# Backward recurrence of a memory transformer: the gradient of O regrouped from SBUF to SBUF, the memory rows' dP in one product, V's part moved to its own block

## The chip, the cores and the metric

One core of a Trainium2 chip. The time is the device time of one execution in microseconds; the time before is the median of three runs.

## The reference, cut to what matters

The kernel returns the output of a block and its gradients with respect to the input, the initial memory, four attention weights and the MLP's weights and biases. The attention part is recurrent: 2048 rows are cut into 64 segments of 32, and each is preceded by 8 memory rows that the segment before has produced.

```python
for s in range(n_seg):                                   # 64
    h = concat([mem, xs[s]], axis=1)                     # 8 + 32 rows of 512
    q, k, v = (einsum('btd,dhe->bhte', h, W) for W in (Wq, Wk, Wv))   # 32 heads of 128
    p = softmax(where(mask, q @ k.T * scale, -1e9))
    o = einsum('bhte,hed->btd', p @ v, Wo)
    mem, out = o[:, :8], o[:, 8:]                        # mem goes into segment s + 1
y = x + out + mlp(layernorm(x))
# returned: y and the gradients by x, mem0, Wq, Wk, Wv, Wo, w1, b1, w2, b2 for a given grad_out
```

The mask lets the 8 memory rows see all 40 rows, and lets row t of the segment see the memory rows and the rows up to its own. In the backward pass the gradient of `mem` goes from segment s to segment s - 1, so the segments run from 63 down to 0, one after another.

## The kernel before

There are four stages: the MLP with its gradients and the layer norm; a first recurrence (forward), up to about 1190 us; a second recurrence (the backward pass of attention), from there to about 2250 us; and the weight gradients with the gradient through the layer norm to the end. The change lies in the second.

**Layout.** A tile has 128 partitions. A "natural" tile (`gN`, `qN`, `kN`, `xs`) has 1024 columns of bf16 and holds four groups of 8 heads: partitions 32j to 32j + 31 are 32 rows (of one segment, or the memory rows of a whole block) for the heads 4i + j, and the columns are 8 heads of 128. Four segments make a block (`SPB` = 4, `TC` = 16 blocks). `s` is a segment, `b = s // 4` its block, `v = s % 4` its place; within a block v runs 3, 2, 1, 0.

**On the chain.** `chain(s)` takes a segment: the gradient of O by the heads, `gN` (projection with Wo, "gO"), its transpose, dP = gO times V (line L1930; V's transpose with the memory's columns is tile `VT`), the softmax's backward pass on VectorE, and three products (`part_bd` 2, 1, 0 for the gradients of V, K and Q), each written to DRAM (`S_GN`) and multiplied by Wv, Wk, Wq into one sum (`dh_part`, L1770). The sum is evicted (`R_A`), and a small matmul (L1985) puts its first 8 rows into the next segment's input `gT`.

**Off the chain.** The queries of the memory rows are handled for the 32 memory rows of a block at once. `l_pre(b)` loads the block's tiles and makes their gradient of O (`gLN`), their dP (L1805, against the memory rows' own keys, tile `VTL`, and the segment's first rows, `VTM`), their softmax gradient (`dSL`, `dSTLL`), and the gradient of Q, which goes to DRAM (`S_GNL[0]`). It is issued when the block before it is at v = 2. `l_post(b)`, issued one block later, reads dQ back, makes the gradients of K (part 1) and V (part 2) and their sum with the weights. For these two it needs rows of all four segments of the block regrouped so that 128 partitions are 4 segments x 32 rows of one head group. That regrouping goes over DRAM: `chain` stores `gN` to `S_GON` (256 KB a segment), and `l_post` loads it back by `quad_rows`, head group by head group, into the four tiles `xs`; it does the same with `S_Q`, and with the padded probabilities `S_PL` and `S_DSL` (64 KB each) into `ys`. Line L1857 multiplies the memory rows' own part, L1870 the regrouped rows.

**Order.** A planner (`_Beat`) writes out the order of all instructions of the recurrence from a table of due times, `_BWD`: one table for the middle blocks, one for the first and one for the last. The numbers decide in which order the operations stand in each engine's queue, and for evictions and copies which engine takes them; nothing waits for a due time itself. Nearly all DMAs of this stage are issued on SP's queue, in the order of the table: an issue that waits holds up those behind it. Many tiles live in parts of larger ones, so the trace shows `XK`, `XN`, `XA`, `XH` for several of the names here (`gN` is in `XA`; the tiles `xs` are in `XN`; `LT0`, `LT1`, the odd `kLN` and `VTL` are in `XK`).

Of the kernel before, what the change touches and what calls it, by code (L numbers as in the profile page):

```python
# [17 lines left out]
P = 128  # L18
# [180 lines left out]
        11817202, 10472800, 15851602, -17692400, -106800, -10764000, 216000, -12492400, 3623200, 6284000, -528797,  # L199
        -546000, -2857200, -480000, -481200, 8879250, 1958400, 3563600, 3428400, 3358800, 10119849, 10143660,  # L200
        10143673, 10758308, 10758321, 6099600, 4994800, 2060400, 541200, 4580802, 7385202, 7385602, 8326802, 8824402,
        9103200, 9060400, 12611600, 12610400, 13626861, 13626873, -4334000, -3086798, -8438400, -12837600, -319597,
        -13471197, -16186000, 938000, 14389648, 14697884, 15015510, 15015520, 15015546, 15015568, 14915540, 14915552,
        14915565, 15155304, 15155317, 16495172, 12582691, 12582703, 14416771, 12582715, 12178775, 12178787, 12178799,
        13008887, 15015532, 15015557, 15015580, 15015593, 15246942, 16495186, 15246952, 15246964, 17158024, 17158036,
        15015664, 15015606, 16401514, 16401526, 16401538, 16401550, 16401562, 16401622, 16495198, 16495210, 17240374,
        17240386, 18255066, 17240398, 18255078, 15015619, 15015631, 15015643, 15015655, 16401575, 16401585, 16401597,
        16401611, 16944336, 16944349, 17240410, 17240423, 17240433, 17240446, 17240456, 17240517, 18235906, 18286922,
        18235916, 18235928, 18286932, 18286944, 23428480, 16401635, 16401645, 16401657, 16401671, 16401681, 16401693,
        16401707, 16401717, 17232288, 17783157, 17240469, 17240481, 17240493, 17240507, 18255090, 18255102, 18255114,  # L210
        18255127, 18255136, 18977533, 18569534, 18977546, 18569544, 18569556, 18977568, 18977580, 18977556, 19690537,
        19782597, 19690548, 19690562, 19782608, 19782622, 24547084, 17535616, 28380764, 13327536, 14420532, 24402643,
        24402655, 22194524, 19977928, -2821228, 7899676, 7373828, 3613352, -4696608, 8571312, 11740568, -69781,
        1558124, 4805860, 6352296, 7315404, 7733381, 10119800, 10119812, 10119824, 10119836, 2902029, 11447020,
        11447032, 11447044, 11447056, 11447070, 11447082, 12669054, 12669066, 13626802, 13626812, 13626824, 13626836,
        13626848, 13626884, 20930640, 20930652, 20930665, 23601096, 23601110, 24402664, 21843516, 21843528, 21843541,
        25147548, 25147561, 26802176, 18255151, 18255163, 23864939, 18255175, 20385003, 19204219, 17240531, 19148035,
        23864948, 23864961, 24748972, 24748985, 24715950, 26802190, 26947188, 27003728, 27104816, 27104828, 24749044,
        24402678, 25646686, 25646698, 25646710, 25646722, 25646734, 25646794, 26802202, 26802214, 26802226, 26802238,
        26802250, 26985338, 26802310, 24748999, 24749011, 24749023, 24749035, 25646747, 25646757, 25646769, 25646783,  # L220
        28361976, 28361989, 26802263, 26802275, 26802285, 26802297, 28614648, 28614661, 28362002, 28614710, 29609052,
        29609064, 29609076, 29609088, 30713416, 25646807, 25646817, 25646829, 25646843, 25646853, 25646865, 25646877,
        25646889, 27878264, 28843061, 27878278, 27878291, 27878301, 27878314, 26802321, 27541630, 26802335, 27083430,
        29000060, 29000073, 28843074, 29000146, 29609100, 29609112, 29609124, 29609136, 29000156, 29609149, 29609161,
        29609172, 29609210, 29609184, 29609222, 29609196, 25929872, 28805088, 21959012, 27793388, 30828719, 30828731,
        28733856, 29000084, 29609232, 29609244, 29609257, 31001308, 32005190, 32005200, 30458968, 31138912, 31138925,
        32272300, 32272313, 33163544, 29000099, 29000111, 29000123, 29000135, 28614675, 28614687, 28614699, 32237603,
        32237612, 32237637, 32237624, 32237649, 33139906, 33315202, 33982864, 33982876, 34779744, 34779756, 32237708,
        32281674, 32281686, 32281698, 32281710, 32281722, 32281734, 32281794, 33163558, 33163570, 33163582, 33163594,
        33810362, 33757294, 33810374, 32237663, 32237675, 32237687, 32237699, 32281747, 32281757, 32281769, 32281783,  # L230
        34296780, 34296793, 33163607, 33163619, 33163631, 33163641, 34923492, 34923505, 34296806, 34923566, 35592576,
        35621428, 35621440, 35621452, 35407824, 32281805, 32281817, 32281831, 32281843, 32359965, 32281853, 32281865,
# [1985 lines left out]
```

## Time and profile before

| | |
|---|---|
| time, median of three runs | 2805.26 us (2798.69 to 2806.51) |
| the profiled execution, its own time | 2806.96 us |
| its span | 2805.2 us |
| TensorE (PE) busy | 2700.5 us, 96% of the span |
| VectorE / ScalarE / GpSimd busy | 1458.3 / 1320.2 / 943.1 us |
| DMA bytes, mean rate | 606.27 MB, 216 GB/s |
| share of SP's hardware queue (q1) | 72.4% of 16 engines' span |

The page's second part cuts the span in 40 slices of 70 us; slices 18 to 32 are the second recurrence. "PEld" is TensorE's weight load, which overlaps the matmuls. A row of a wait reads: who waited, on which line, for whom, then the total in us, how often, and the longest. A row of the timeline reads: start, length, engine, line, operation, tiles written and read, count, and in brackets the idle time before it and what ended it.

### The profile page before, as it was taken

Reading aid. Unit: us, or ns where it says so; the run is one execution under the profiler, and the core shown is the slowest. Engines: PE = TensorE matmul, PEld = TensorE weight load, DVE = VectorE, ACT = ScalarE, POOL = GpSimd, SP = SyncE. Lnnn points to the kernel's source line nnn. Section 1 sums busy time; section 2 is a strip of 40 time slices with the busy share of each in tenths; the row PEclk is TensorE's granted clock in tenths of the full one; section 3 lists DMA queues with packets and bytes.
Section 4 is the critical chain, followed back from the end, with each engine's and each line's share of the span. In section 5 each row is a group of like instructions: output and inputs, shape, how many; then the busy total and the mean of one; then the engine's idle time right before and its main releaser. Section 6 shows DMA issues by size and latency. Waiting matters only on the chain.

```text
span 2805.2 us, 114167 instructions
## 1 busy us (share of the span) xinstructions
PE 2700.5 (96%) x47681; PEld 1554.6 (55%) x47681; DVE 1458.3 (52%) x4384; ACT 1320.2 (47%) x3149; POOL 943.1 (34%) x2638
## 2 busy tenths in 40 slices
PE   8999999999999999899999999999999899999999
PEld 6665555665566665665555555555555444444444
DVE  5555655555565655665656555555655402232322
ACT  4333565556565565556666666666666400000000
POOL 1102233333333333344544445454544301112211
PEclk9999999999999999999999999999999999999999
DMA  7657677877787774468999999999999898788861
GB/s 214 208 167 220 194 202 205 212 208 205 198 216 210 199 204 158 137 167 218 234 232 241 236 235 232 238 232 234 228 238 222 243 342 278 232 254 270 257 185 40
DMA packets 556392, 606.27 MB, mean 216 GB/s; under 512 B 228145, under 2 KB 357442, under 8 KB 553826
## 3 DMA queue, kind: packets, MB, share of 16 engines
q1 hardware_dynamic: 540706, 544.88, 72.4%
q0 software_dynamic: 15168, 54.08, 6.1%
q8 instruction: 374, 6.13, 1.0%
q14 instruction: 144, 1.18, 0.2%
HBM read 290.14 MB, written 272.12 MB: 200 GB/s over the span
## 4 chain that ended last, share of the span: by engine, by line
PE 48%; DMA 5%; issue 2%; DVE 2%; ACT 2%; SPq 0%; POOL 0%; POOLq 0%; DVEq 0%; ACTq 0%
PE ps L2155 14%; PE ps L1770 13%; PE ps L976 6%; PE ps L866 6%; PE ps L2158 4%; PE ps L752 3%; DMA S_GN<-XK 2%; DMA S_GON<-XA 1%; PE ps L1985 1%; PE ps L1870 1%; DMA WA<-S_GN 1%; PE ps L1930 1%; PE ps L932 1%; ACT XN L758 1%; PE ps L1857 0%
## 5 line engine op out<-in xcount | busy, mean ns | idle before, releaser
L866 PE MATMUL ps<-WA,PA 128*32 128x512 bf16 x6144 | 366.1, 379 | 4.7 <-DVE PA L1596 2.7
L2155 PE MATMUL ps<-WA,WB 128*128 128x512 bf16 x1536 | 332.3, 379 | 0.6 <-DVE gwo L756 0.6
L1770 PE MATMUL ps<-WA,XK 128*32 128x512 bf16 x5120 | 307.9, 382 | 6.5 <-DVE XK L849 6.3
L2155 PEld LDWEIGHTS <-WB 128*128 128x128 bf16 x1896 | 185.5, 98 | 224.8 <-issue 1.3
L866 PEld LDWEIGHTS <-PA 128*32 128x32 bf16 x8192 | 200.1, 96 | 194.2 <-DVE PA L1596 14.4
L992 POOL COPY BDA<-PB 32x128 bf16<-32x128 bf16 x600 | 172.8, 288 | 370.2 <-DVE PB L1566 268.4
L758 ACT CAST gwo<-ps 128x512 bf16<-128x512 f32 x64 | 33.2, 599 | 517.7 <-PE ps L2155 357.9
L758 ACT CAST XK<-ps 128x512 bf16<-128x512 f32 x379 | 211.0, 588 | 85.5 <-PE ps L976 65.2
L756 DVE CAST gwo<-ps 128x512 bf16<-128x512 f32 x64 | 40.0, 684 | 402.6 <-PE ps L2155 268.4
L1770 PEld LDWEIGHTS <-XK 128*32 128x32 bf16 x5120 | 123.1, 97 | 142.4 <-DVE XK L849 26.7
L1770 PE MATMUL ps<-WA,XN 128*32 128x512 bf16 x2560 | 173.4, 380 | 2.7 <-DVE XN L849 2.2
L2166 POOL DMA_DIRECT2D out_dram<-gwo x96 | 71.4, 751 | 296.6 <-ACT gwo L758 265.0
L758 ACT COPY XN<-ps 128x256 f32<-128x256 f32 (+2 forms) x227 | 100.8, 473 | 130.1 <-PE ps L1770 122.8
L758 ACT CAST XA<-ps 128x512 bf16<-128x512 f32 x143 | 83.4, 589 | 156.0 <-PE ps L866 131.9
L866 PE MATMUL ps<-WB,PA 128*32 128x512 bf16 x2048 | 132.5, 381 | 7.5 <-DVE PA L1988 4.3
L1648 PE MATMUL ps<-XA 128*128 128x512 bf16 x448 | 131.3, 381 | 3.3 <-DMA XA<-S_GT 2.2
L849 DVE STREAM_TRANSPOSE XK<-XK 128x256 f32<-128x256 f32 x256 | 112.0, 442 | 42.8 <-ACT XK L758 37.2
L1435 PE MATMUL ps<-WB,OT 128*32 128x256 bf16 x4096 | 132.5, 276 | 1.8 <-DVE OT L849 1.3
L998 POOL COPY BDA<-XA 32x256 bf16<-32x256 bf16 x256 | 104.5, 408 | 54.4 <-ACT BDA L992 17.7
L976 PEld LDWEIGHTS <-XK 128*128 128x128 bf16 x1536 | 94.0, 98 | 48.0 <-issue 18.0
L1435 PEld LDWEIGHTS <-OT 128*32 128x32 bf16 x4096 | 101.2, 97 | 32.6 <-DVE OT L849 19.3
L992 POOL COPY BDB<-PB 32x128 bf16<-32x128 bf16 x228 | 65.7, 288 | 157.8 <-DVE PB L1567 149.1
(310 smaller groups left out, 5467.2 us busy)
## 6 DMA issues: line engine op xcount, KB each, us to landing
S_GN<-XK SPq DMA_DIRECT2D x192, 256.0 KB
WA<-S_GN SPq DMA_DIRECT2D x160, 256.0 KB
S_Q<-qN SPq DMA_DIRECT2D x64, 256.0 KB
S_K<-kN SPq DMA_DIRECT2D x64, 256.0 KB
S_V<-vN SPq DMA_DIRECT2D x64, 256.0 KB
S_ON<-oN SPq DMA_DIRECT2D x64, 256.0 KB
XA<-S_K SPq DMA_DIRECT2D x64, 256.0 KB
XA<-S_Q SPq DMA_DIRECT2D x64, 256.0 KB
```

The source lines that it names most:

```text
L752: nc.tensor.transpose(ps_ap, in_ap, ident[base:base + k, base:base + k])
L758: nc.scalar.copy(out, in_)
L849: self.plan.add({"DVE": 0.36}, lambda e, x=x: nc.vector.transpose(dst[:, x, :, :].rearrange("p i c r -> p (i c r)").bitcast(F32).rearrange ...
L866: nc.tensor.matmul(bk()[32 * j:32 * (j + 1), :], lhsT=win(dc), rhs=Wt(dc, c0), start=(dc == 0), stop=(dc == DC - 1), tile_position=(0, 32 ...
L976: nc.tensor.matmul(bv()[:, n * P:(n + 1) * P], lhsT=B_[:, i, :, :].rearrange("p j k -> p (j k)"), rhs=X[:, i, :], start=(y == 0 and n == 0 ...
L992: self.plan.add({"ACT": 0.31, "DVE": 0.2, "POOL": 0.31}, lambda e, j=j: {"ACT": nc.scalar.copy, "DVE": nc.vector.tensor_copy, "POOL": nc.g ...
L998: self.plan.add(cost or {"ACT": 0.4, "DVE": 0.27, "POOL": 0.42}, lambda e, j=j: {"ACT": nc.scalar.copy, "DVE": nc.vector.tensor_copy, "POO ...
L1435: nc.tensor.matmul(bk()[32 * t:32 * (t + 1), :], lhsT=tq(OTt, i, j), rhs=Wo[:, JQ * i + j, h * HB:(h + 1) * HB], start=(i == 0 and j < 2), ...
L1648: A(pe(0.217, "f", 0.11), lambda e, c=c, z=z, x=x: nc.tensor.matmul(bks[x]()[:], lhsT=anT[x][:, c, :], rhs=sx[z][:], start=(c == 0), stop= ...
L1770: nc.tensor.matmul(bk()[32 * j:32 * (j + 1), :], lhsT=tq(XT, i, j), rhs=wtf(t, i, j), start=(first and i == 0), stop=(last and i == NI - 1 ...
L2155: nc.tensor.matmul(bks[n]()[:], lhsT=HNc[:, rc, dc * P:(dc + 1) * P], rhs=half_of(gns[y], hf), start=(y == 0), stop=(y == NRC - 1))
L2158: nc.tensor.matmul(bks[n]()[:], lhsT=gns[y][:, k * P:(k + 1) * P], rhs=GOc[:, rc, :], start=(y == 0), stop=(y == NRC - 1))
```

## The change

1. **The gradient of O, regrouped from SBUF to SBUF.** The DRAM tensor `S_GON` is gone. At the end of each segment four DMAs copy the four head groups of `gN` (32 partitions, 64 KB each) straight into partitions 32v to 32v + 31 of four tiles `xg`. `l_post`'s part 2 reads these. `xg` takes two of the tiles that were `xs` and two new ones, so `xs` has two tiles instead of four, used twice each for part 1. The rows of `S_PL` are loaded in the matching order (segment, row).
2. **dP of the memory rows in one product.** `VTL` and `VTM` lie beside each other and are read as one operand `VLM`; 32 matmuls with 64 columns take the place of 64 with 32.
3. **Where the parts stand.** `l_pre` is cut in pieces. `l_soft` (loads of `VTL` and `VTM`, dP, softmax gradient) is issued ahead of the last segment of the block before; `l_keys` (load of `kLN`) behind that segment; `l_query` (load of `KM`, dQ) behind the block's own first segment, and dQ's transpose is taken from the tile, not read back from DRAM. `VTL` and `kLN` have one buffer each instead of two. V's part, `l_post(b, 2)`, is issued at the end of its own block, K's part with the sum one block later, as before.
4. **A new table** `_BWD` of due times for all three kinds of block; the constant `_BWD_BEAT` is the same.

```diff
-    S_GON = dt_([TC, P, SPB, HW], BF16, "S_GON")
...
-        VTL, kLN = [tr4(XK[0], 2 * HW), tl("VTL", TR)[:]], [nat(XK[0], 4 * HW), tl("bkLN", NAT)[:]]
+        VTL, kLN = tr4(XK[0], 2 * HW), nat(XK[0], 4 * HW)
         LT0, LT1, LT2 = tr4(XK[1]), tr4(XK[0], 3 * HW), tr4(XN[3])
         VTM = LT1
+        VLM = XK[0][:, 2 * HW:4 * HW].rearrange("p (c i j r) -> p i j c r", c=2, i=NI, j=JQ)
...
-        xs = [XN[x] for x in (1, 4, 5, 7)]
-        btL = xs[3][:].bitcast(F32).rearrange("p (i k) -> p i k", i=NI)
+        xs = [XN[x] for x in (1, 4)]
+        xg = [XN[5], XN[7], tl("xg2", [P, HW]), tl("xg3", [P, HW])]
+        btL = xs[1][:].bitcast(F32).rearrange("p (i k) -> p i k", i=NI)
...
         def l_pre(b):
-            dmaT(lambda: trv(VTL[p]), lambda: S_VL[b], [], [("VTL", p)])
-            dmaT(lambda: trv(VTM), lambda: S_VM[b], [], both("LT1"))
-            sg.dma(lambda: flat(kLN[p]), lambda: S_KL[b], [], [K("kLN")], lat=3.0)
-            sg.dma(lambda: flat(KM), lambda: S_KM[b], [], both("dLN"), lat=3.0)
...
-            sg.to_T_plain("f", "gLT", gLN[p], K("gLN"), LT0, "LT0", 1)
...
-                    for c, VX in enumerate((VTL[p], VTM)):
-                        for j in range(JQ):
-                            nc.tensor.matmul(q_(bk(), j)[:, i, 32 * c:32 * c + 32], lhsT=LT0[:, i, j, :],
-                                             rhs=VX[:, i, j, :], start=(i == 0 and c == 0), stop=True,
-                                             tile_position=(0, 32 * j), skip_group_check=True)
...
+            sg.to_T_plain("f", "gLT", gLN[p], K("gLN"), LT2, "LT2", 1)
+
+        def l_soft(b):
...
+            dmaT(lambda: trv(VTL), lambda: S_VL[b], [], ["VTL"])
+            dmaT(lambda: trv(VTM), lambda: S_VM[b], [], both("LT1"))
...
+                    for j in range(JQ):
+                        nc.tensor.matmul(q_(bk(), j)[:, i, :].rearrange("p (c k) -> p c k", c=2), lhsT=LT2[:, i, j, :],
+                                         rhs=VLM[:, i, j], start=(i == 0), stop=True,
+                                         tile_position=(0, 32 * j), skip_group_check=True)
...
+            smax_bwd("L", bk, 2 * RL, PLL[p], K("PLL"), dSL[p], K("dSL"), 1, 0.71)
...
+        def l_keys(b):
+            sg.dma(lambda: flat(kLN), lambda: S_KL[b], [], ["kLN"], 0, lat=3.0)
+
+        def l_query(b):
+            sg.dma(lambda: flat(KM), lambda: S_KM[b], [], both("dLN"), lat=3.0)
+            sg.diag_own("f", [
+                (lambda r, i: q_(dSTLL, r)[:, i, 0, :], lambda r, i: q_(kLN, r)[:, i, :]),
+                (lambda r, i: q_(dSTLL, r)[:, i, 1, :], lambda r, i: q_(KM, r)[:, i, :]),
+            ], ["dSTLL", "kLN"] + both("dLN"), ("dLN", dLN), 1, True)
+            sg.dma(lambda: part_of(S_GNL[0], b, BPC), lambda: flat(dLN), both("dLN"), [])
             sg.sq_T(dLN, "dLN", LT0, "LT0", 1)
...
+                if t == 2:
+                    xx, xk = [x[:] for x in xg], [[("xg", j, v) for v in range(SPB)] for j in range(JQ)]
+                else:
+                    xx, xk = [xs[j % 2][:] for j in range(JQ)], [[("xs", 0)], ["btL"]] * 2
...
-                    sg.dma(lambda: xx[r], lambda: quad_rows(big, b, r),
-                           [(bn, s) for s in range(b * SPB, b * SPB + SPB)], xk[r], lat=3.2)
-                    sg.dma(lambda: yy[r], lambda: quad_rows(pad, b, r),
+                    if t == 1:
+                        sg.dma(lambda: xx[r], lambda: quad_rows(big, b, r), [], xk[r], lat=3.2)
+                    sg.dma(lambda: yy[r], lambda: quad_rows(pad, b, r) if t == 1 else pad[b, 32 * r:32 * (r + 1)].rearrange("r v f -> v r f"),
...
         def chain(s):
-            sg.dma(lambda: part_of(S_GON, s, SPB), lambda: flat(gN), both("gN"), [("S_GON", s)])
+            for r in range(JQ):
+                sg.dma(lambda r=r: xg[r][RA * v:RA * (v + 1), :], lambda r=r: flat(gN)[RA * r:RA * (r + 1), :], both("gN"), [("xg", r, v)], lat=3.0)
...
                 if v == SPB - 2 and b > 0:
                     l_pre(b - 1)
+                if v == 0 and b > 0:
+                    l_soft(b - 1)
                 chain(s)
                 sg.rings = {}
+                if v == 0 and b > 0:
+                    l_keys(b - 1)
                 if s > 0:
                     load(s - 1)
-                if v == SPB - 1 and b + 1 < TC:
-                    l_post(b + 1)
+                if v == SPB - 1:
+                    if b + 1 < TC:
+                        l_post(b + 1, 1)
+                    l_query(b)
+            l_post(b, 2)
             blk_out(b)
-        l_post(0)
+        l_post(0, 1)
```

More of the change, by code (lines that the diff above doesn't have):

```diff
@@ new lines, in l_soft @@
+            for y in range(4):
+                A(pe(0.11, "w"), lambda e, y=y: dp(e, y), both("LT2") + both("LT1") + ["VTL"], [bk.key])
+            smax_bwd("L", bk, 2 * RL, PLL[p], K("PLL"), dSL[p], K("dSL"), 1, 0.71)
+            A({"DVE": 0.72}, lambda e: V.transpose(dSTLL[:].rearrange("p i c k -> p (i c k)"), flat(dSL[p])),
+              [K("dSL")], ["dSTLL"])
+        def l_keys(b):
+            plan.at = (TC - 1 - b, 0)
+            sg.dma(lambda: flat(kLN), lambda: S_KL[b], [], ["kLN"], 0, lat=3.0)
@@ L2020 @@
         l_pre(TC - 1)
+        l_soft(TC - 1)
+        l_keys(TC - 1)
         pl = TC % 2
```

51 lines of the change are left out of this document (21 added, 30 removed), and 339 rows, old and new, of the table _BWD.

## The prediction

> **What bounds the kernel now.** I read the page first, then busy time by windows cut at the block borders of the second recurrence, then waits, DMA, and the timeline around the edited steps.
>
> ```profile
> span 2805.2 us, 114167 instructions
> PE 2700.5 (96%) x47681; PEld 1554.6 (55%) x47681; DVE 1458.3 (52%) x4384; ACT 1320.2 (47%) x3149; POOL 943.1 (34%) x2638
> DMA  7657677877787774468999999999999898788861
> ```
>
> TensorE is busy 96% of the span, and the DMA row stands at 8 to 9 tenths from slice 19 on, which is where the second recurrence begins. All of the change lies there. A block of it is four segments; each ends with the small matmul L1985 that hands the gradient to the next one, so I cut the windows at the L1985 that ends segment 0 of each block. In order: best block, worst block, sum of the twelve middle blocks; the last full block, the three segments after it, and a stretch of the weight-gradient phase.
>
> ```profile
> core 0: us, PE busy (x) PEld busy (x) DVE busy (x) ACT busy (x) POOL busy (x), PEclk, DMA share, GB/s
> 1592.59:1654.45 61.86, 60.32 (x1394) 35.25 (x1388) 37.20 (x118) 39.84 (x98) 31.19 (x98) 1.00 0.93 243
> 1654.45:1718.71 64.26, 60.84 (x1396) 35.07 (x1389) 37.51 (x119) 39.28 (x97) 31.21 (x98) 1.00 0.88 225
> sum 758.34, PE 728.84 PEld 424.42 DVE 448.45 ACT 475.88 POOL 374.74; mean PE 60.74 PEld 35.37 DVE 37.37 ACT 39.66 POOL 31.23
> ...
> 2098.73:2164.07 65.34, 61.18 (x1394) 35.09 (x1388) 37.65 (x119) 39.48 (x97) 29.45 (x95) 1.00 0.97 227
> 2250.00:2280.00 30.00, 30.00 (x138) 13.49 (x137) 0.00 (x0) 0.40 (x1) 0.56 (x1) 0.98 1.05 385
> ```
>
> The twelve blocks take 758.34 / 12 = 63.20 us on average, the best one 61.86, with the same work (1394 to 1396 matmuls). So about 60.7 us a block is matmul work, 1.5 us is idle time that even the best block has, and 1.34 us is excess that comes and goes. Only the first term, the work, and the last, the excess, can be touched by edits that lie off the chain. Where does the excess come from?
>
> ```profile
> ACT XA L758 <- DMA S_GON<-XA: 8.7, 3, 3.7
> POOL BDA L998 <- DMA XN<-S_GON: 10.0, 8, 1.3
> PE ps L1985 <- ACT XN L758: 11.4, 24, 0.5
> PE ps L866 <- issue: 2.2, 3, 1.1
> PE ps L752 <- ACT XA L758: 1.7, 2, 1.3
> ```
>
> These are waits (us in total, times, longest) over the twelve blocks. L1985 waiting for its eviction is chain latency and stays. But the eviction of gN (tile XA) waited 8.7 us for the store of the old gN to S_GON, and TensorE's transpose L752 behind it lost 1.7 us. L866 stood 2.2 us on "issue", inside one run of matmuls, for nothing the profile shows. Next, the DMA engines over the same twelve blocks.
>
> ```profile
> DMA packets 191191, 177.72 MB, mean 234 GB/s; under 512 B 96049, under 2 KB 123665, under 8 KB 191011
> q1 hardware_dynamic: 191011, 175.18, 94.1%
> XN<-S_GON SPq DMA_DIRECT2D x48, 256.0 KB
> S_GON<-XA SPq DMA_DIRECT2D x48, 256.0 KB
> dLN<-S_GNL SPq DMA_DIRECT2D x12, 256.0 KB
> ```
>
> SP's queue keeps the sixteen engines 94.1% occupied: nearly as full as TensorE. A transfer that has to land by a given moment has little room.
>
> **The change part by part.** *dP of the memory rows.* 64 matmuls of 32 columns become 32 of 64 columns.
>
> ```profile
> 1766.12 0.59 PE L1985 MATMUL ps<-sel,XN 128*32 128x8 f32 x32 [0.48 <-ACT XN L758]
> ...
> 1772.12 0.28 PE L1930 MATMUL ps<-XA,XN 128*32 128x40 bf16 x16
> 1772.24 1.03 PE L1770 MATMUL ps<-WA,XN 128*32 128x512 bf16 x16
> ...
> 1774.85 0.19 PE L1805 MATMUL ps<-VTL,XK 128*32 128x32 bf16 x4
> ...
> 1775.45 0.40 PE L976 MATMUL ps<-bqLN,XK 128*128 128x128 bf16 x4
> ...
> 1782.08 0.44 PE L1985 MATMUL ps<-sel,XN 128*32 128x8 f32 x32
> ```
>
> L1805 holds TensorE from 1774.85 to 1775.45, 0.60 us for 64, or 37 ns for each four that run side by side. The 16 matmuls of 40 columns (L1930) took 0.12 us, 30 ns for four: wider costs no more here. So half as many cost half: 0.30 us saved, on the bounding engine, 16 times: 4.8 us. Ends: 0 (if the columns, which stay the same in number, set the cost) and 0.35.
>
> *The detour over DRAM.* Out per block: four stores of gN to S_GON, four loads of it, one reload of dLN, nine transfers of 256 KB. In: sixteen copies of 64 KB from gN straight into xg. In the weight phase the engines moved 385 GB/s at a share of 1.05, or 367 GB/s when full, so 256 KB is 0.71 us of all engines. That takes out 6.4 us and puts in 2.9: 3.5 us less of 63.2, and the 94.1% falls to about 88.5%. No row shows a copy between two SBUF tiles; a price per byte between half and twice this leaves 5.0 to 0.7 us. I take the same price, since 2 KB rows move in both. What it saves in time lies between 0 and the whole excess of 1.34 us a block. The eviction row names a removed transfer for 8.7 / 12 = 0.7 us a block, of which only 1.7 / 12 = 0.14 is seen to reach TensorE, and the issue gaps come on top: I take 0.5 us, over 15 blocks 7.5 us. The last full block stands 65.34 - 61.86 = 3.5 us over the best; I take 1.5 of it.
>
> *SP's queue.* Nine issues out and sixteen in, seven more a block.
>
> ```profile
> 1793.57 0.39 SPq L812 DMA_DIRECT2D S_GON<-XA  x1
> ...
> 1813.57 1.29 SPq L1777 DMA_TRANSPOSE XK<-S_VM  x1
> ...
> 1860.94 1.87 SPq L812 DMA_DIRECT2D bkLN<-S_KL  x1
> ```
> ```profile
> SPq L812 <- ACT XK L758: 46.2, 72, 1.7
> ```
>
> At 0.39 us that is 2.7 us more of SP per block. SP waits 46.2 / 12 = 3.9 us a block in its longest row alone, so I cost it at nothing; without that cover it delays what is queued behind, the loads of the next segment's V, P, q and k, by 3 x 0.39 = 1.2 us a segment. The copies add two waits: for gN's eviction, as the S_GON store did, and for the matmuls that read xg a block earlier, which is long past.
>
> *V's part at its block* (l_soft). The transposes of VTL and VTM, dP, the softmax gradient and its transpose move from segment 2's place to segment 0's; the counts on SP, DVE and TensorE stay. VTL has one buffer, so its transpose waits for GpSimd's copy for segment 0, and SP's later issues stand behind it. In the trace dP already runs in segment 0 (1774.85 lies between the two L1985 rows, the borders of that segment), so dSL is ready about when it was: nothing.
>
> *kLN* (l_keys) also has one buffer, loaded after its last reader. *The query part* (l_query) moves behind segment 3 with its KM load, its eviction and its store, and goes on from dLN without the round trip: the same matmuls, no cost. *xs* has two buffers, so the third and fourth S_Q loads wait for the first half of L1870's matmuls: off the chain, 0 in the steady part.
>
> *The tail.*
>
> ```profile
> 2215.70 6.51 DMA S_GON<-XA
> ...
> 2229.86 9.05 DMA WB<-S_HNA
> ...
> 2240.50 4.44 DMA S_GNL<-dLN
> ```
> ```profile
> 2232.90 1.91 PE L1770 MATMUL ps<-WA,XN 128*32 128x512 bf16 x32 [1.10 <-DVE XN L849]
> ...
> 2239.48 0.62 PE L1870 MATMUL ps<-XN,XN 128*32 128x128 bf16 x16 [1.32 <-DMA XN<-S_DSL]
> 2241.97 1.04 PE L1870 MATMUL ps<-XN,XN 128*32 128x128 bf16 x16 [1.86 <-DMA XN<-S_DSL]
> 2246.16 3.60 PE L1770 MATMUL ps<-WA,XK 128*32 128x512 bf16 x32 [3.15 <-DVE XK L849]
> ```
>
> The chain holds the S_GON store of the last segment (6.51 us), behind which SP's loads wait, and the S_GNL store of dLN (4.44 us), which keeps the second eviction of dLN waiting. Both leave this place: part 2 is done before the end. TensorE's four gaps are 1.10 + 1.32 + 1.86 + 3.15 = 7.43 us. Late next is the second pair of S_Q loads on two buffers, one landing of 4.4 us or more between the two L1870 rows. Ends: 7.4 gained, 4.4 lost; I take 2.5 gained.
>
> *The new table* reorders everything, and no row prices it. Blocks of the same work under one table spread over 64.26 - 61.86 = 2.4 us; half of that either way, 1.2 us x 15 = 18 us, bounds it. I take 0.
>
> Sum: 4.8 + 7.5 + 1.5 + 2.5 = 16.3 us off. The profiled execution took 2806.96 us (span 2805.2 and 1.8 around it), which gives 2790.7; the median of the three runs, 2805.26, stands 1.7 us lower, so I say 2789.
>
> **The rivals.** *No relief.* The copies could occupy the engines twice as long as their bytes say, or the excess could stem from something else; then the 0.5 us a block and the 1.5 us go, and 4.8 + 2.5 = 7.3 us remain: 2798; with a table half a microsecond a block worse it is about 2805. For it: blocks with a share of 0.93 and of 0.88 are the best and the worst one, so share alone does not order the blocks. Against it: the S_GON rows above. [...]
>
> *Everything recovered.* The whole excess goes: 4.8 + 15 x 1.34 + 3.5 + 5 = 33 us: 2772. For it: two of the rows of waits name transfers that go. Against it: the largest row that TensorE itself shows off the chain is issue, which names none.
>
> *Slower: kLN comes too late.*
>
> ```profile
> 1778.06 0.40 PE L976 MATMUL ps<-XK 128*128 128x128 bf16 x4
> ...
> 1791.39 0.40 PE L976 MATMUL ps<-bkLN,XK 128*128 128x128 bf16 x4
> ```
>
> The last matmuls on the old kLN are at 1778.5, the first on the next block's at 1791.4, 12.9 us later. Into this gap the load must now fit: an issue of up to 1.87 us and a landing between the 4.4 and the 9.05 us seen above, 6.3 to 10.9 us, on a queue in which other waits stand ahead. It holds if SP comes to it within 2 us; each microsecond beyond goes into the chain of every block. At 2 us late the fifteen blocks lose 30 us: 2789 + 30 = 2819. The point from which it decides is 1.65 us a block: 15 x 1.65 = 24.7 us lead from 2789 to 2813.7, which is 0.3% over the median.
>
> **How the numbers follow.** 0.3%, 8.4 us, is about what a measurement of this kernel can tell from no change. Forecast 0.45 (own range 2780 to 2796), everything recovered 0.12, no relief 0.23 (2797 to 2813), slower 0.20 (2814 and up). Faster is the first two, 0.57; within 0.3% is the third, 0.23; slower 0.20. The range 2770 to 2816 leaves out most of the slower case and the best of the second.
>
> **What would show it.** dP's line at 32 matmuls a block and about 0.3 us; q1 near 88% over the middle blocks; no S_GON; blocks averaging 62.4 us, with the worst ones nearer the best; TensorE's gaps between the last segment and the weight phase near 5 us. The prediction is wrong if the best block of the new order is longer than 61.6 us, if a part 0 product waits for kLN, or if gN's eviction waits longer for four copies than it did for one store.

## The result, and the profile after

The changed kernel takes 2834.07 us (median of four runs, 2832.72 to 2834.95) against 2803.19 us of the kernel before on the same chip: the ratio is 1.0107 (95% interval 1.0093 to 1.0121). It is slower by 30.9 us, where 2789 us was predicted; the time lies outside the predicted range of 2770 to 2816 us. The profiled execution took 2834.59 us.

The same rows of the page as before:

```profile
span 2832.8 us, 113609 instructions
PE 2703.7 (95%) x47169; PEld 1551.2 (55%) x47169; DVE 1509.2 (53%) x4443; ACT 1297.8 (46%) x3102; POOL 941.3 (33%) x2626
DMA  7657777877778764558888888898788899788861
```

TensorE has 512 matmuls fewer and yet is busy 3.2 us longer. The DMA row has fallen by a tenth in much of the second recurrence, as wanted. Cut at the line that ends segment 0 (L1985 before, L1997 now), the 27.6 us between the two spans are: 8.9 us up to the first border, -1.2 us over the next seven segments, 17.4 us over the twelve middle blocks, 1.8 us in the last full block, 3.0 us in the three segments after it, -2.3 us in the tail. The windows of the blocks (best, one that will be looked at, worst, sum; then the last full block):

```profile
core 0: us, PE busy (x) PEld busy (x) DVE busy (x) ACT busy (x) POOL busy (x), PEclk, DMA share, GB/s
1476.34:1538.80 62.46, 60.18 (x1364) 35.05 (x1357) 40.35 (x123) 38.26 (x94) 31.29 (x98) 1.00 0.86 213
1538.80:1604.09 65.29, 61.82 (x1364) 36.00 (x1356) 40.48 (x123) 38.34 (x94) 31.47 (x98) 0.97 0.81 206
...
2054.92:2123.93 69.01, 62.00 (x1364) 35.83 (x1356) 41.14 (x123) 38.25 (x94) 31.26 (x98) 0.98 0.87 197
sum 775.75, PE 730.87 PEld 422.09 DVE 486.72 ACT 458.55 POOL 375.68; mean PE 60.91 PEld 35.17 DVE 40.56 ACT 38.21 POOL 31.31
...
2123.93:2191.03 67.10, 60.68 (x1365) 34.48 (x1357) 40.59 (x123) 38.28 (x94) 28.86 (x92) 1.00 0.86 208
```

A block takes 64.65 us where it took 63.20; the best one 62.46 where it was 61.86. Of the 17.4 us, 15.4 are time in which TensorE stands idle (44.9 us against 29.5), and 2.0 are more busy time of TensorE. By place in the block it is one segment that loses: segment 3 went from 15.63 to 18.59 us, while segment 2 became 1.4 us shorter and 1 and 0 moved by 0.3.

For what does TensorE wait? The waits over the twelve blocks, after:

```profile
ACT XK L756 <- DMA S_GN<-XK: 48.4, 32, 3.2
POOL XA L1916 <- DMA XA<-S_V: 34.5, 12, 4.0
PE ps L1770 <- DVE XK L847: 11.5, 11, 2.4
PE ps L1879 <- DMA XN<-S_Q: 7.6, 11, 2.1
PE ps L750 <- ACT XA L756: 7.2, 16, 1.9
```

and the first of them in the kernel before:

```profile
ACT XK L758 <- DMA S_GN<-XK: 7.4, 13, 1.3
```

ScalarE may not evict the next gradient into tile XK while the store of the last one to `S_GN` is still reading it. This wait grew from 7.4 to 48.4 us, VectorE's transpose (L847) waits behind it and TensorE's L1770 behind that, for 11.5 us. The loads come late as well: S_Q for K's part (7.6 us of TensorE), and V (34.5 us of GpSimd, 8.4 before). The stores have not become slower to land: those for which ScalarE waited took 6.28 us from issue to landing before and 4.75 after (medians). They are issued late. SP's queue around one of these places, then ScalarE, VectorE and TensorE (start, length, engine, line, operation, tiles; in brackets the idle time before and its releaser):

```profile
1545.08 1.27 SPq L1777 DMA_TRANSPOSE PA<-in_grad_out_dram  x1
1546.45 0.54 SPq L810 DMA_DIRECT2D XN<-XA  x1
1547.05 1.22 SPq L810 DMA_DIRECT2D xg<-XA  x2
1548.36 1.66 SPq L810 DMA_DIRECT2D S_GN<-XK  x1
```
```profile
1553.08 1.07 ACT L756 CAST XK<-ps 128x512 bf16<-128x512 f32 x2 [3.19 <-DMA S_GN<-XK]
```
```profile
1553.70 0.93 DVE L847 STREAM_TRANSPOSE XK<-XK 128x256 f32<-128x256 f32 x2 [3.21 <-ACT XK L756]
```
```profile
1554.20 0.62 PE L1770 MATMUL ps<-WA,XK 128*32 128x512 bf16 x8 [2.42 <-DVE XK L847]
```

Three of the new copies (`XN<-XA`, `xg<-XA`) and a transposing load stand back to back ahead of the store, 3.0 us of issuing. The store goes out at 1548.36 (its own issue takes 1.66 us), and TensorE idles for 2.42 us up to 1554.20.

That stall has a second price. The window behind it:

```profile
1553.00:1558.00 5.00, 3.38 (x46) 2.10 (x50) 2.35 (x5) 1.66 (x3) 1.57 (x4) 0.67 1.01 262
```

The granted clock falls to 0.67 in this window: the trace records a stretch of 3.4 us at half rate from 1554.7. There are four such stretches in the twelve blocks and none in the kernel before, and three of them begin within 0.6 us of the end of a gap of 1.98 to 2.42 us (a gap of 2.13 us was followed by none). The trace shows more: its ten half-rate stretches, over the whole span, begin whole multiples of 3.413 us after one another. In the 3.413 us just ahead of each of the four TensorE was idle for 1.89 to 2.42 us in all, in any other such interval of the twelve blocks for 1.73 us at most (in the kernel before, 1.24 us at most). The gap of 2.13 us lay across the border of two intervals.

The four blocks concerned have 61.79 us of busy TensorE on average, the other eight 60.46; so about 4 x 1.33 = 5.3 us of the 17.4 are clock (an estimate), and without them TensorE would be busy for less time than before.

### The profile page after: what moved, and what is told of

Read it like the earlier page. It is cut to its first block, busy times and chain, and to the rows that moved or that the text cites. A ratio compares the mean times of both kernels' runs of the same rounds, so it can differ in the third digit from the quotient of the medians.

```text
span 2832.8 us, 113609 instructions
## 1 busy us (share of the span) xinstructions
PE 2703.7 (95%) x47169; PEld 1551.2 (55%) x47169; DVE 1509.2 (53%) x4443; ACT 1297.8 (46%) x3102; POOL 941.3 (33%) x2626
## 5 line engine op out<-in xcount | busy, mean ns | idle before, releaser
L1770 PE MATMUL ps<-WA,XK 128*32 128x512 bf16 x5120 | 322.8, 384 | 14.5 <-DVE XK L847 13.2
L756 ACT CAST XK<-ps 128x512 bf16<-128x512 f32 x339 | 194.1, 588 | 99.4 <-DMA S_GN<-XK 56.7
L1770 PEld LDWEIGHTS <-XK 128*32 128x32 bf16 x5120 | 129.7, 97 | 139.3 <-DVE XK L847 33.9
L756 ACT COPY XN<-ps 128x256 f32<-128x256 f32 (+2 forms) x266 | 123.0, 487 | 164.7 <-PE ps L1770 120.3
L1770 PE MATMUL ps<-WA,XN 128*32 128x512 bf16 x2560 | 174.5, 384 | 1.2 <-DVE XN L847 1.0
L756 ACT CAST XA<-ps 128x512 bf16<-128x512 f32 x155 | 91.3, 590 | 121.3 <-PE ps L864 103.0
L847 DVE STREAM_TRANSPOSE XK<-XK 128x256 f32<-128x256 f32 x256 | 108.5, 436 | 47.9 <-ACT XK L756 42.7
L990 POOL COPY BDB<-maskA 32x128 bf16<-32x128 bf16 x228 | 67.5, 296 | 160.5 <-DVE maskA L1968 154.3
```

What stands on the lines that cost most here:

```text
L756: nc.scalar.copy(out, in_)
L847: self.plan.add({"DVE": 0.36}, lambda e, x=x: nc.vector.transpose(dst[:, x, :, :].rearrange("p i c r -> p (i c r)").bitcast(F32).rearrange ...
L990: self.plan.add({"ACT": 0.31, "DVE": 0.2, "POOL": 0.31}, lambda e, j=j: {"ACT": nc.scalar.copy, "DVE": nc.vector.tensor_copy, "POOL": nc.g ...
L1770: nc.tensor.matmul(bk()[32 * j:32 * (j + 1), :], lhsT=tq(XT, i, j), rhs=wtf(t, i, j), start=(first and i == 0), stop=(last and i == NI - 1 ...
```

## The experiments

Theory: SP's queue. SP issues 71.9 DMAs a block before and 79.0 after, and its instructions fill 69.7% and 81.1% of the time; the chain's own stores stand in the same queue and come late. Rivals: the bytes of the copies on the DMA engines; the two buffers of the Q part (`xs`), whose third and fourth loads wait; the new table by itself. "Blocks" below is the mean of the twelve middle blocks.

**Issues without bytes, in the kernel before.** Four copies of 32 rows x 64 B a segment to one scratch tile, behind the S_GON store:

```diff
+  for r in range(JQ):
+      nc.sync.dma_start(scr[RA * v:RA * (v + 1), :], flat(gN)[RA * r:RA * (r + 1), 0:32])
```

> The kernel before, with four tiny copies more in each segment, issued on SP right behind the S_GON store: 32 rows of 64 bytes from gN into a scratch tile that nobody reads. Issue theory (SP's queue is what the new copies cost: 0.58 us an issue in the profile after, 81% of the time against 70%): 16 x 0.55 = 8.8 us of SP a block more, as much as in the change, so S_GN stores go out later and the time rises by 12 to 25 us over before. [...] Table theory (the new order costs): no change.

Measured: 3219.62 us, ratio 1.1502 (1.1482 to 1.1521). A miss of design: all four write the same bytes, so each waited for the one before to land.

```profile
SPq L2002 <- DMA scr<-XA: 212.7, 105, 5.0
```

212.7 / 105 = 2.0 us each. It says nothing about issues alone, but it shows that SP's waiting goes into the chain. Repeated with copies of 16 B a row that write different bytes (`scr[RA * v:RA * (v + 1), r]`):

> The kernel before with four tiny copies a segment more on SP (32 rows of 16 bytes, each to bytes of its own, so that none waits for another; nobody reads them). Issue theory: 16 x 0.51 = 8.1 us of SP a block and no load of the engines: 10 to 30 us over before. [...]

Measured: 2871.53 us, ratio 1.026 (1.0234 to 1.0287); blocks 67.91 us, 4.7 more, 0.29 us for each tiny copy; SP occupied 83.1%. The wait of the changed kernel appears in the old one, with the old table (here from 1400 us to 2060):

```profile
ACT XK L758 <- DMA S_GN<-XK: 41.1, 31, 3.0
```

**The copies out, in fewer issues, or half of them.** In the changed kernel: no copies, with `xg` zeroed once; one DMA of all 128 partitions a segment in place of four; the copies of r = 0 and 2 alone. All three leave out rows of a weight gradient (that of Wv) or put them in the wrong place, so they serve for the time alone.

```diff
-  sg.dma(lambda r=r: xg[r][RA * v:RA * (v + 1), :], lambda r=r: flat(gN)[RA * r:RA * (r + 1), :], ...)
+  # no copies: nothing; one copy (r == 0 only):
+  sg.dma(lambda: xg[v][:], lambda: flat(gN), both("gN"), [("xg", r, v)], lat=3.0)
```

> The changed kernel without the copies of gN into xg (part 2 of the memory rows is computed from zeros). Issue theory: SP loses 16 issues, 10 us a block; the wait of the part 0 eviction for the S_GN store (48.4 us in twelve blocks) falls to the 7.4 us of before, and the time falls by 15 to 25 us from 2834, to 2809 to 2819. Buffer theory (the S_Q loads on two xs tiles cost): S_Q's waits remain, and the time stays within 6 us of 2834. Table theory: within 6 us of 2834.

> The changed kernel with one copy of 256 KB and 128 partitions a segment in place of four of 64 KB and 32 partitions (the rows land in the wrong places, so part 2 of the memory rows is not the reference's). Same bytes, 12 issues a block fewer. Issue theory: three quarters of what no_copy gains, 11 to 19 us off 2834. Copy theory by bytes: nothing gained. [...] Table theory: within 6 us of 2834.

> The changed kernel with the copies of r = 0 and 2 alone (71 issues a block; the other two buffers are zeroed once, so their part of the gradient is left out). No work is put on another engine in exchange, so against the kernel with half of the copies by VectorE (65.42 us a block, 71 issues) it separates SP's part from VectorE's. If SP's harm begins near 80% of its time, the blocks are at 61.7-62.3 and the time at 2788-2798. If it is proportional to the copies, they are at 63.1 and the time at 2808-2813. If 65 again, neither the count nor VectorE explains that kernel.

| | issues a block | SP occupied | DMA share | blocks | time | ratio (interval) |
|---|---|---|---|---|---|---|
| no copies | 63 | 64.4% | 80.6% | 61.61 | 2787.57 | 0.9954 (0.9939 to 0.9969) |
| one copy, same bytes | 67 | 67.4% | 87.4% | 61.67 | 2797.34 | 0.998 (0.9967 to 0.9993) |
| half of the copies | 71 | 73.5% | 84.9% | 62.64 | 2798.09 | 0.9997 (0.9981 to 1.0013) |
| the change | 79 | 81.1% | 85.8% | 64.65 | 2834.07 | 1.0107 (1.0093 to 1.0121) |

ScalarE's wait for the stores in these three, from 1400 to 2060 us, where the change has 34.8 us:

```profile
ACT XK L757 <- DMA S_GN<-XK: 3.1, 2, 1.9
ACT XK L757 <- DMA S_GN<-XK: 8.5, 12, 1.6
ACT XK L756 <- DMA S_GN<-XK: 6.5, 8, 2.1
```

Bytes are not it: with the same bytes in a quarter of the issues, at a higher DMA share than the change has, the time is 36.7 us below the change's. Against no copies, bytes and four issues together cost 9.8 us by the medians, or 0.6 us a block (0.06 in the profiled execution, which was this kernel's fastest, 2788.26 us). Issues are: the first eight cost 1.0 us a block, the next eight 2.0, or 0.13 and 0.25 us each. So in these kernels the cost is neither a plain price nor a threshold; it grows as SP fills. Most of it falls on segment 3, where the new table puts the most issues (24.2 of the 79, 20.1 in the kernel before): 16.56, 17.46 and 18.59 us with none, half and all. With no copies, the new table's blocks are 1.6 us shorter than the old one's 63.20, and with one copy, which moves all the bytes, 1.5 us. Both have less traffic than the detour of before, so this does not price the table alone; it shows that the table's blocks are no slower when SP has room.

**Another place in SP's order.** The copies 4 us later, behind the store of `S_GN`.

> The changed kernel with its four copies of a segment put 4 us later in the order, so that in SP's order they stand behind the store of gN's second half (S_GN of part 2) instead of ahead of it. The count stays 79 issues a block. If only the place of the copies does the harm (they stand ahead of a store for which ScalarE's and VectorE's evictions wait), the waits ACT XK L756 <- DMA S_GN<-XK (48.4 us in 48 segments) fall back to about 10 and the blocks from 64.65 to about 62, the time to about 2795-2805. If it is the count (SP has 81% of its time in issues and falls behind wherever the copies stand), the same wait turns up behind other transfers and the blocks stay at 64-65, the time at 2825-2840.

Measured: 2915.59 us, ratio 1.0413 (1.0382 to 1.0444); blocks 69.70. Worse than both forecasts.

```profile
ACT XA L757 <- DMA XN<-XA: 38.9, 7, 7.1
ACT XK L757 <- DMA S_GN<-XK: 34.8, 22, 5.5
```

The second wait is as large as in the changed kernel over the same window (34.8 us in 24), and a new one has come: the copies read gN, and the next eviction into its tile XA waits for them. This place is no way out.

**Another queue or engine.** The copies issued by ScalarE (`eng="ACT"`) or GpSimd (`eng="POOL"`); or done by VectorE, all four, with the old split of the evictions ahead of the first block, half of them, or all four later in the order:

```diff
+  A({"DVE": 0.4}, lambda e, r=r: V.tensor_copy(xg[r][RA * v:RA * (v + 1), :], flat(gN)[RA * r:RA * (r + 1), :]), ...)
```

> The changed kernel, the sixteen copies a block issued on ScalarE's queue, in their place in its order, instead of on SP. [...] Issue theory: SP has the 63 issues a block of the run without copies, so blocks fall from 64.65 towards its 61.61 us; ScalarE (39 of 63 us busy) takes the issues, and what it loses on the chain is the open price: 0 to 1.5 us a block, so 2788 to 2815. [...]

> The same on GpSimd's queue. Issue theory: SP is relieved as well; GpSimd's own issue is dearer (751 ns for an output in the weight phase) and it fills the block diagonals on the chain, 16 x 0.75 = 12 us a block on an engine that is busy for 31 of 63: 2790 to 2830. [...]

> The changed kernel with the regrouping done by VectorE: four tensor copies of 32 partitions x 1024 bf16 a segment in place of the four copies by DMA. SP's issues go from 79 to 63 a block, the DMA share to about that of the kernel with no copies (80.6%). VectorE is busy 63% of the middle stretch and gets about four times 0.3-0.5 us a segment (estimate from 437 ns for its 128x256 f32 transposes, 678 ns for its 128x512 evictions), so goes to 71-75%. SP's theory: the blocks return to 61.6-62.5 us and the time to 2788-2803 (no copies at all: 61.61 and 2787.6). If a rival held in which it is the order of the new table rather than SP, or if the VectorE copies stand in the chain's way as the issues did on ScalarE's queue, the blocks stay at 64 or more and the time at 2825 or more.

> The same as the kernel with VectorE's copies, and the evictions of the transposed weights ahead of the first block are given to VectorE and ScalarE 22 to 14 as in the kernel before (29 to 7 in the new table). If this split is what made the stretch ahead of the first chain 4.7 us longer, the first border comes about 4-5 us earlier and the time falls by as much against that kernel, to about 2784-2798. If the stretch has another limit, the two are alike within 2 us.

> The changed kernel with half of the regrouping by VectorE (r = 1 and 3) and half by DMA on SP's queue (r = 0 and 2): 71 issues a block, as many as the kernel before has (71.9). SP's theory: the waits of the evictions for S_GN are about those of the kernel before (7 us in 48 segments), the blocks at 61.7-63, the time 2790-2808, between the kernel with four copies by DMA (64.65) and the kernel with none (61.61), and nearer to the latter since the harm begins near 80% of SP's time. If the harm is proportional to the number of copies, the blocks are at 63.1.

> The kernel with VectorE's copies, the four put 1.5, 2.0, 2.5 and 3.0 us later in the order, so that VectorE doesn't stand waiting for gN's second half (DVE XN L2011 <- ACT XA L756: 57.5 us in 28 waits) while the chain's own work queues behind it. If that waiting is what costs the 4.7 us a block over the kernel with the copies by DMA (69.37 against 64.65), the blocks fall to 62-65 us and the time to 2795-2840. If it is the 0.42 us of each copy in the chain's way, or gN's buffer held longer, they stay above 66.5 us and the time above 2860.

| the copies on | blocks | time | ratio (interval) |
|---|---|---|---|
| ScalarE's queue | 71.69 | 2934.85 | 1.048 (1.0448 to 1.0513) |
| GpSimd's queue | 74.93 | 2985.19 | 1.0667 (1.0639 to 1.0696) |
| VectorE | 69.37 | 2898.38 | 1.0352 (1.0332 to 1.0371) |
| VectorE, old split of the first evictions | 69.00 | 2900.72 | 1.0352 (1.0333 to 1.037) |
| VectorE two, SP two | 65.42 | 2842.04 | 1.0152 (1.0133 to 1.0171) |
| VectorE, 1.5 to 3 us later | 68.08 | 2886.56 | 1.0313 (1.0285 to 1.0341) |

SP was relieved in all of them (63 or 71 issues), and all are slower. The first waits of ScalarE's and GpSimd's version, and VectorE's copies:

```profile
PE ps L1942 <- ACT XN L756: 58.7, 37, 2.9
```
```profile
PE ps L974 <- POOL XK L996: 49.7, 27, 2.9
```
```profile
L2011 DVE COPY xg<-XA 32x1024 bf16<-32x1024 bf16 x76 | 32.2, 423 | 1.7
L2011 DVE COPY XN<-XA 32x1024 bf16<-32x1024 bf16 x75 | 31.0, 414 | 58.3 <-ACT XA L756 57.5
```

An engine of the chain that issues a copy (on ScalarE's queue, from 1700 to 1730 us, 0.51 and 0.53 us for one, 1.16 and 1.26 us for two in a row, 1.32 us for one more) or waits for gN ahead of it holds up its evictions, and TensorE stands for them. Issued by ScalarE and by GpSimd, the copies cost 10.1 and 13.3 us a block against no copies, where SP's queue cost 3.0. Against no copies, VectorE's sixteen cost 69.37 - 61.61 = 7.8 us a block, 0.49 each; eight, against the kernel with the other eight by DMA, 65.42 - 62.64 = 2.8 us, 0.35 each. Taking away most of VectorE's wait for gN (57.5 us, then 7.5) gained only 1.3 us, and TensorE's L1770 stood behind VectorE almost as long as before: 15.6 + 11.6 + 11.0 us, then 35.7. The sizes fit each copy's own 0.42 us standing in the chain's way nearly in full, although VectorE is busy only 63% of the time in the changed kernel; that gN's tile is held longer was not tested apart. The old split of the first evictions left the first border where it was (1239.99 and 1240.62 us): that theory for the late start is not borne out.

**The reloads of the Q part.** Its third and fourth loads of `S_Q` left out, so that half of K's part is made from the wrong rows; or issued 4 us earlier, with the second product that reads them 4 us later.

> The changed kernel without the third and fourth S_Q load of each block (the second half of part 1's products uses the first half's rows). Buffer theory: TensorE's waits for S_Q go (7.7 us in the middle blocks, 6.5 us at the end) and what follows them in segment 3; the time falls by 10 to 18 us from 2834. Issue theory: two issues a block fewer, 0.9 us of SP, so 1 to 4 us off. Table theory: nothing beyond 4 us.

> The changed kernel with new due times for part 1 alone: the third and fourth S_Q load 4 us earlier (right behind the products that free their two tiles) and the products that need them 4 us later. Buffer theory: it is the order around the reload that costs, so TensorE's waits for S_Q and S_DSL (11 us in twelve blocks, 6.5 us at the end) go: 2805 to 2822. Issue theory: SP's count stays, so at most 8 us off 2834; earlier loads push the S_GN stores behind them, so it may be none.

Left out: 2802.85 us, ratio 1.0014 (1.0004 to 1.0023), blocks 63.46, the tail 585.53 us instead of 590.88. Moved: 2835.65, 1.0131 (1.0101 to 1.0161), blocks 65.60. Leaving out two loads regains 31 us, so they are no free work; 5.0 us of it, however, lie ahead of the first border, and 14.3 in the twelve blocks. Moving them regains nothing.

**The detour over DRAM restored, the rest of the change kept.** One store of gN a segment and four loads a block, just ahead of the loads of PL; then moved 5 to 9 us later; the same with `xs` on four buffers (two of `xg`); then placed 7.2 to 8.1 us behind the block's last store.

```diff
+  sg.dma(lambda: part_of(S_GON, s, SPB), lambda: flat(gN), both("gN"), [("S_GON", s, 0)], lat=3.0)
...
+  sg.dma(lambda: xx[r], lambda: quad_rows(S_GON, b, r), [("S_GON", s, 0) for s in ...], xk[r], lat=3.2)
```

> The changed kernel with the regrouping undone: gN goes to DRAM by one store a segment in the place of the first copy, and the four loads of a block (as in the kernel before, and with the rows of PL loaded in that order too) stand just ahead of the four loads of PL. dP in one product, V's own block and the new table stay. 71 issues a block instead of 79. SP's theory: blocks of 61.7-62.7 us and 2788-2805 us, since 63 and 67 issues gave 61.6-61.7; the copies alone then carry the loss. If the buffers reloaded for the gradient of Q, or the table, carry a part of the loss, the blocks stay above 63.5 and the time above 2815.

> The kernel with the regrouping undone, its four loads of S_GON moved 5, 6, 8 and 9 us later in the order (the product that reads them starts some 12 us after them). In the kernel without this move the first load stood at the head of SP's queue until its own store had landed (SPq L814 <- DMA S_GON<-XA: 32.1 us in 12 waits), and gN's stores behind it kept ScalarE and VectorE from evicting (v0 20.18 us instead of 15.2). If that wait is all that cost 5 us a block there, v0 returns to 15.2-15.6 and the blocks to 62.4-63 us, the time to 2793-2806: no loss against the kernel before, with dP in one product, V's own block and the new table kept. If the loads' traffic or the table costs, the blocks stay above 64 and the time above 2820.

> The same, and the third and fourth loads of the gradient of Q's block go into two of the four buffers of gN, which lie idle at that time (their loads come some 45 us later), and are due 4 us earlier; so they no longer wait for the first product to free the two shared buffers. Leaving these loads out gained 1.2 us a block and 5.4 us at the tail in the changed kernel. If the waiting for the shared buffers caused that, this kernel comes out at 2775-2792, 5 to 20 us ahead of the one without it and ahead of the kernel before; if it was the issues and bytes of the loads, the two are alike within 3 us.

> The kernel with the regrouping undone, its four loads of S_GON now placed by their own store: due 7.2 to 8.1 us behind the last store of the block in the order. The move by 5 to 9 us before was too small, since the places of these loads lie 10 to 38 us ahead of the last store: there the loads still stood directly behind it and the wait stayed (SPq L815 <- DMA S_GON<-XA: 31.1 us in 10 waits, v0 19.86 us). If that wait is the whole loss of that kernel, v0 now returns to 15.2-15.6 us, the blocks to 62.3-63.0, the time to 2793-2806, so the rest of the change (dP in one product, V's own block, the new table) is neutral against the kernel before. If the table or the rest of the change costs by itself, v0 is still the odd one with another wait, the blocks above 64 and the time above 2820.

| S_GON's loads | blocks | segments 3 and 0 | time | ratio (interval) |
|---|---|---|---|---|
| ahead of PL's | 67.75 | 17.56, 20.18 | 2871.49 | 1.0261 (1.0236 to 1.0286) |
| 5 to 9 us later | 67.44 | 17.69, 19.86 | 2872.70 | 1.0257 (1.0233 to 1.0281) |
| so, and `xs` on four buffers | 68.96 | 18.69, 20.41 | 2896.78 | 1.0352 (1.0329 to 1.0376) |
| behind the last store's landing | 65.19 | 19.47, 15.63 | 2842.69 | 1.0137 (1.0118 to 1.0156) |

All have 71 issues, and all missed the 62 to 63 us a block that the count promised. In the first, the count is not what hurts:

```profile
SPq L814 <- DMA S_GON<-XA: 32.1, 12, 4.2
```
```profile
ACT XK L760 <- DMA S_GN<-XK: 67.8, 25, 5.4
```

Once a block a load waits at the head of SP's queue for its own store to land, 2.7 us, and the chain's stores wait behind it. The second run moved the loads too little to leave that place. The last one did (its profiled execution, 2854.75 us, was its slowest), and segment 0 came back to 15.63 us; but now the loads lie among those of segment 3, which went to 19.47 us, and the same wait is there again:

```profile
ACT XK L764 <- DMA S_GN<-XK: 38.5, 23, 3.3
PE ps L1895 <- DMA xg<-S_GON: 2.8, 4, 1.2
```

So in none of the places tried does the detour with this table reach the kernel before. Whether it would with a table made for it was not tried. None of the versions that keep the whole computation beats the kernel before.

## Why the prediction was wrong, point by point

*The step that failed is SP's queue*, "I cost it at nothing", with its 2.7 us a block covered by SP's waiting. Size: SP is occupied 44.1 us a block before and 52.4 after, 8.4 us more. A copy's issue took 0.645 us on average (median 0.58), not the 0.39 of the S_GON store, and the stores of `S_GN` went from 0.445 to 0.594 us on average. Cover: the row that was to provide it is now

```profile
SPq L810 <- ACT XK L756: 9.9, 23, 1.0
```

instead of 46.2 us. That SP waits a lot in total does not mean that it waits at the moment at which four issues arrive. Behind: the prediction looked at the loads of the next segment; the stores of `S_GN`, whose tile the chain wants back, stand there too. The tiny copies in the kernel before and the one copy with the same bytes show the cause.

*dP*, 4.8 us: mis-sized. The timeline of the new product and of what follows it:

```profile
1663.89 0.42 PE L1807 MATMUL ps<-XK,XN 128*32 128x64 bf16 x32
1664.40 1.05 PE L1770 MATMUL ps<-WA,XK 128*32 128x512 bf16 x16
```

It holds TensorE for 0.51 us (median of the blocks 0.50), against 0.60: 0.10 us saved, 1.6 us over sixteen blocks. The matmuls themselves start as fast as was taken, four every 29 ns. What was missed comes after them: the next line's first matmul starts 0.28 us after the last of these (0.15 and 0.18 in two blocks), where it was 0.12 us. Why, stays open.

*The detour over DRAM*, 7.5 + 1.5 us: the relief of the DMA engines came, and more of it than said. Over the twelve blocks:

```profile
DMA packets 183458, 162.07 MB, mean 209 GB/s; under 512 B 95806, under 2 KB 123454, under 8 KB 183278
q1 hardware_dynamic: 183278, 159.55, 84.4%
XN<-XA SPq DMA_DIRECT2D x96, 64.0 KB
xg<-XA SPq DMA_DIRECT2D x96, 64.0 KB
```

84.4% instead of 94.1% (88.5% were expected), and the waits for S_GON are gone. But the one-copy kernel at 87.4% is 36.7 us faster than the change at 85.8%, and at 80.6% only 9.8 us more are gained, so the share was little of what the blocks lacked. What the change can give without the copies' issues shows in the kernel with no copies: 63.20 - 61.61 = 1.6 us a block (1.5 with one copy), three times the 0.5 that was taken, and given back by the issues. No run shows the doubled price of the rival *no relief*. With the copies on ScalarE's own queue (q10), from 1400 us to 2200,

```profile
q1 hardware_dynamic: 161750, 135.75, 67.2%
q10 hardware_dynamic: 8640, 11.81, 6.7%
```

the copies took 0.067 x 16 x 800 / 11.81 = 72.6 us of an engine per MB, the other transfers 63.4. The others include small packets. By their bytes 5760 of the 8640 packets of q10 are of 2 KB; with the other 2880 at 14 ns, the mean of the 4 B packets in the changed kernel, one of 2 KB took 142 ns (an estimate), where in the kernel before it took 105.4 ns on average: 1.35 times as much, not twice. Against the 43.6 us per MB of the price taken (367 GB/s), 72.6 is 1.7 times.

*xs on two buffers*, "0 in the steady part": it holds only while SP has room. From 1400 to 2060 us TensorE waits for S_Q for 6.4 us in the change, but for 1.0 and 0.8 us with no copies and with one, on the same two buffers. Leaving two loads out of the change gains 1.2 us a block. Whether that is the wait for the buffer or the two issues is not shown: earlier loads and four buffers did not help, though the four buffers were tried in a kernel that lost by another wait.

*The tail*, 2.5 us gained: 2.3 measured, but with other gaps inside than named. The "late next" was real and is now the largest gap:

```profile
2272.89 0.26 PE L1879 MATMUL ps<-XN,XN 128*32 128x128 bf16 x1 [6.05 <-DMA XN<-S_Q]
...
2275.63 2.75 PE L1770 MATMUL ps<-WA,XK 128*32 128x512 bf16 x24 [1.05 <-DVE XK L847]
```

*The last full block* did not get shorter by 1.5 us but longer by 1.8. *The table*, 0: no row prices it alone; its blocks are shorter than the old ones when SP has room, its start is longer. *kLN*, the slower rival: no wait for it shows; the loss came by another way, one that the prediction had named and priced at nothing. *The start*: 8.9 us up to the first border were not foreseen. 4.2 of them are there at the last segment of the forward pass, which the change does not touch; that point scatters from 1180.7 to 1188.0 us among the profiled executions with the new table. The other 4.7 lie in the stretch of the transposed weights up to the border: 47.5 us before, 52.2 after, 52.2 or more in every run with the new table and 47.8 or less in the three with the old. So they come with the change; by what, stays open.

One sum of the prediction is off: its parts of a block, 60.7 + 1.5 + 1.34 us, add up to 63.5, not 63.20, since the idle time is the best block's and the work the mean. The excess of 1.34 us, which the later terms use, is right.

Of its own signs, two told: the best block is longer than 61.6 us, and dP's line has 32 matmuls but 0.50 us. The third, gN's eviction waiting for the copies, did not come; it was the store behind the copies that was waited for.

## What to carry to other kernels

Cost a DMA by three things: its bytes, its issue on the queue, and what stands behind it in that queue; splitting one transfer into four small ones costs four issues (sixteen copies of 16 B a row cost the kernel before 4.7 us a block), and where the chain's own stores go through a queue that is already 70% occupied, each further issue can cost the chain: here 0.13 to 0.29 us. Slack in total is no cover: look for the wait that stands at the very place into which the work is put. And before moving issues to another engine, see whether that engine's evictions are on the chain: here the same copies cost 10.1, 7.8 and 13.3 us a block on ScalarE, VectorE and GpSimd, and 3.0 on SP.

## What the runs showed of the hardware

- Issuing a copy from SBUF to SBUF of 32 partitions and 2 KB a row held SP for 0.51 us at least in the changed kernel (median 0.58); a store of gN to DRAM in the kernel before 0.32 in the median. Sixteen copies more a block of 16 B a row cost the kernel before 0.29 us each. The issue of the loads of PL went from 0.43 to 0.59 us in the median when their rows were read in the copies' order.
- In the changed kernel the granted clock was half for 3.413 us four times in the twelve blocks. In the 3.413 us ahead of each TensorE was idle for 1.89 to 2.42 us, in any other interval of the same grid for 1.73 us at most. In the kernel before it was 1.24 us at most, with no such stretch. With VectorE's copies the granted clock over the twelve blocks was 0.98 on average, before the change 1.00.
- 32 matmuls of 64 columns in four column groups took 0.50 us up to the first matmul of the next line (median of the twelve blocks), 64 of 32 columns 0.60. Within them four started every 29 ns, and every 25 to 33 ns.
